# Splitting the first K products by contraction half, freeing the K/V banks later, reordering two down sets and raising a planner's latencies in a fused attention and SwiGLU kernel

## Chip, cores and metric

One core of one Trainium2 chip. The metric is the device time of one execution, in microseconds (us). Each kernel was run several times and timed beside the kernel before on the same chip. The profile is one traced execution; its span is about 1.7 us shorter than the time reported for that run.

## The reference

```python
x = A_x                                     # [1, 2048, 1024] bf16
xn = _layernorm(x)                          # no scale, no bias
s = linear_attention(xn, A_wqkv) @ A_wo     # 32 heads of 32; phi(t) = t+1 if t>0 else exp(t), + 1e-6
                                            # kv = sum phi(k) v, z = sum phi(k), o = phi(q) kv / (phi(q) z)
g = silu((silu(xn @ w_gate) * (xn @ w_up)) @ w_down)     # inner width 3584
return x + s * g
```

## The kernel before

The kernel is written as a list of operations with their reads and writes. A small planner simulates the five engines and emits each engine's instructions in the order in which they would start in that simulation. An engine then executes its list strictly in order. So a constant of the planner, such as a latency, changes no arithmetic, but it changes who stands in front of whom in each queue.

The large products are done by a seven-product scheme on half blocks (steps 1 to 7 below), with sums and differences of blocks made by VectorE (DVE); results leave the PSUM banks through DVE or ScalarE (ACT). The stages in order are: K and V products of 16 row tiles with the K/V sums accumulated in three PSUM banks; then two passes over half of the rows each, with query sets, gate/up sets and four down sets. A down set interleaves the steps D of the feed-forward product with the steps S of the attention product. S needs a 512 KB slice of the attention matrix, which is reloaded from DRAM for each down set into a single buffer.

```python
LAT = {"pe": 0.22, "act": 0.2, "dve": 0.2, "pool": 0.2}     # planner: result visible this late
...
def mm_cost(mms):
    return sum(max(r.shape[-1] / 2400.0 + 0.0012, 0.03) for (_, _, r, _, _) in mms)
...
# tile i: bn_stats x2, aggr, +eps on DVE; rstd on Pool; normalise on DVE for i < 2, on ACT after that
# t_tile(0): eight transposes on PE, first half copied out by ACT, second half by DVE:
if q == 0:
    act([bank_r[b]], [xr], dst[:, k0:k0 + n], pb, ACT.Identity)
else:
    dve([bank_r[b]], [xr], lambda h, ...: h.tensor_copy(dst[:, k0:k0 + n], pb), n * 128)
...
def p_piece(i, w, j):                       # one K or V product of row tile i: 8 matmuls of 512 columns
    b = balloc()
    mms = [(ps[b][:, :], xt_ap(i, kt), KVV[w]["R%d%d" % (kt // 4, j)][0][:, kt % 4, :], kt == 0, kt == KT - 1)
           for kt in range(KT)]
    pe_mm([xt_r(i), KVV[w]["R0%d" % j][1], KVV[w]["R1%d" % j][1]], [bank_r[b]], mms)
...
for n, (fn, args) in enumerate(((x_load, (0,)), (x_load, (1,)), (wkv_load, (0, 1)), (wkv_load, (0, 0)),
                                (x_load, (2,)), (wkv_load, (1, 1)), (x_load, (3,)), (wkv_load, (1, 0)))):
    ...                                     # wkv_load(w, j) asks for two blocks of 512 KB
...
def m_load(c):                              # slice c of the attention matrix, always into the same place
    raw = W.at(MR, 4 * KB, FP16)...
    dma([named("mscr", c // 2)], [rr], raw, m_v[:, :, c * 256:(c + 1) * 256], dsem("mld"), 512 * KB)
...
if first:                                   # down set c == 0
    seq = "D1 D5 D6 D2 D7 S1 S5 D3 S2 S6 D4 S7 S3 S4"
else:
    seq = "S1 S5 S2 S6 D1 S7 S3 D5 S4 D6 D2 D7 D3 D4"
...
# first query set of the first pass: kv_done re-arms the three K/V banks by writing to them with PE
q_pair(p, n, st, ((1, kv_done), (9, kvt)) if (p, n) == (0, 0) else ())
```

Of the kernel before, what the change touches and what calls it, by code (L numbers as in the profile page):

```python
# [14 lines left out]
KB = 1024  # L15
# [15 lines left out]
class Plan:  # L31
# [1 line left out]


    ENGS = ("pe", "act", "dve", "pool", "sp")
    LAT = {"pe": 0.22, "act": 0.2, "dve": 0.2, "pool": 0.2}

    def __init__(self, window, lead):
        self.ops = []
# [180 lines left out]
def build_kernel(nc, A_x, A_wqkv, A_wo, B_w_gate, B_w_up, B_w_down, out, WINDOW=6, NWARM=14, NPE=4, LEAD=12.0):  # L220
    S, D, FF = 2048, 1024, 3584
    NT, KT, NG, NPAIR = 16, 8, 8, 14
# [4 lines left out]
    wqkv_v = A_wqkv.rearrange("(kt p) c -> p kt c", p=128)  # L227
# [5 lines left out]
    with ExitStack() as es:  # L233
# [70 lines left out]
        MM = 0.2137  # L304

        def mm_cost(mms):
            return sum(max(r.shape[-1] / 2400.0 + 0.0012, 0.03) for (_, _, r, _, _) in mms)

        def pe_mm(reads, writes, mms):
            return PL.op("pe", reads, writes, partial(_mm_group, mms), mm_cost(mms))  # L310
# [220 lines left out]
            xslot[i] = s  # L531
            dma([], [s.r], s.ap(), xf[i * 128:(i + 1) * 128, :], dsem("x%d" % s.k), 256 * KB).urgent = 10.0

        def wkv_load(w, j):
            for k in range(2):
                ap, r = kvblock(w, KB_OF[k, j])
                c0 = 1024 * (1 + w) + j * 512
                dma([], [r], ap, wqkv_v[:, 4 * k:4 * k + 4, c0:c0 + 512], dsem("wkv%d%d%d" % (w, j, k)), 512 * KB)

        xnslot = {}  # L540

# [102 lines left out]

        def p_piece(i, w, j):
            b = balloc()
            mms = [(ps[b][:, :], xt_ap(i, kt), KVV[w]["R%d%d" % (kt // 4, j)][0][:, kt % 4, :], kt == 0, kt == KT - 1)
                   for kt in range(KT)]
            pe_mm([xt_r(i), KVV[w]["R0%d" % j][1], KVV[w]["R1%d" % j][1]], [bank_r[b]], mms)
            if w == 0:  # L650
                k_evac(i, j, ps[b][:, :], bank_r[b], "ps")
            else:
                v_evac(i, j, ps[b][:, :], bank_r[b])
            bfree(b)
# [47 lines left out]
                st.direct = direct  # L702
            return st

        for n, (fn, args) in enumerate(((x_load, (0,)), (x_load, (1,)), (wkv_load, (0, 1)), (wkv_load, (0, 0)),
                                        (x_load, (2,)), (wkv_load, (1, 1)), (x_load, (3,)), (wkv_load, (1, 0)))):
            k = len(PL.ops)
            fn(*args)
            for o in PL.ops[k:]:
                o.urgent = 60.0 - 2 * n  # L710
        ln_tile(0)
        t_tile(0)
        ln_tile(1)
        p_piece(0, 0, 1)
        t_tile(1)
        p_piece(1, 0, 1)
        x_load(4)
        x_load(5)
        p_piece(0, 0, 0)
        ln_tile(2)  # L720
        p_piece(1, 0, 0)
        t_tile(2)
        combos(KVV[0])
        p_piece(0, 1, 1)
        ln_tile(3)
        p_piece(1, 1, 1)
        t_tile(3)
        combos(KVV[1])
        p_piece(0, 1, 0)
        for b in tb:  # L730
            rearm(b)
        p_piece(1, 1, 0)
        fill = deque([partial(a_tile, 0), partial(a_tile, 1)])
        stats_of = {1: x_sums(1)}
        todo = [(u, w) for u in range(1, NT // 2) for w in range(2)]
# [310 lines left out]

        out_evs = []

        def d_set(p, c, Sx, mstat, first):
            gv, sv, xo = {}, {}, {}  # L1050

            def fin(i, j):
                if (i, j) not in gv or (i, j) not in sv:
                    return
                g, s = gv[i, j], sv[i, j]
                tt([g.r, s.r], [g.r], g.ap(FP16), g.ap(FP16), s.ap(FP16), ALU.mult, True)
                row = p * 1024 + j * 512
                if j not in xo:
                    q = xo_ring.take()
                    xo[j] = (q, [])  # L1060
                    xv = q.ap().rearrange("p (m n) -> p m n", n=256)
                    dma([], [q.r], xv, xf[row:row + 512, c * 256:(c + 1) * 256].rearrange("(m p) n -> p m n", p=128),
                        dsem("xo%d" % q.k), 256 * KB)
                q, seen = xo[j]
                xv = q.ap().rearrange("p (m n) -> p m n", n=256)

                def done():
                    seen.append(i)
                    if len(seen) == 2:
                        dma([q.r], [], of[row:row + 512, c * 256:(c + 1) * 256].rearrange(  # L1070
                            "(m p) n -> p m n", p=128), xv, dsem("oo%d" % q.k), 256 * KB)

                def turn_dma():
                    o = pt_ring.take()
                    oa = o.ap(FP16).rearrange("p (m n) -> p m n", n=128)
                    PL.op("sp", [g.r], [o.r], lambda h: h.dma_start_transpose(oa, g.ap(FP16)), 0.08,
                          sem=dsem("tp%d" % o.k), nbytes=200 * KB)
                    tt([o.r, q.r], [q.r], xv[:, :, i * 128:i * 128 + 128], oa, xv[:, :, i * 128:i * 128 + 128], ALU.add,
                       True)
                    done()  # L1080

                def turn():
                    if not tbank:
                        tbank.append(balloc())
                    b = tbank[0]
                    pb = ps[b][:, 0:256].bitcast(FP16).rearrange("p (m n) -> p m n", n=128)
                    pe_tr([g.r, ident_r], [bank_r[b]], [(pb[:, m, :], g.ap(FP16)[:, m * 128:(m + 1) * 128], ident[:, :])
                                                           for m in range(4)])
                    tt([bank_r[b], q.r], [q.r], xv[:, :, i * 128:i * 128 + 128], pb[:, :, :],
                       xv[:, :, i * 128:i * 128 + 128], ALU.add)  # L1090
                    done()
                if (p, c) == (1, 3):
                    defer(2, turn)
                else:
                    turn_dma()

            def keep(store, func):
                def f(i, j, ap, r, bank):
                    s = fin_ring.take()
                    store[i, j] = s  # L1100
                    act([r], [s.r], s.ap(FP16), ap, func, "ps" if bank is not None else "sb")
                    fin(i, j)
                return f

            def dops(m):
                wv, wr = Sx[m]
                parts = []

                def with_t4():
                    for n in range(0, NPAIR, 2):  # L1110
                        t = t4_ring.take()
                        tv = t.ap(FP16).rearrange("p (n t) -> p n t", t=512)
                        r10, t2 = hb2(n, "R10"), hb2(n, "T2")
                        tt([r10[1], t2[1]], [t.r], tv, r10[0], t2[0], ALU.subtract, True)
                        yield [(wv[:, n + q, :], tv[:, q, :]) for q in range(2)], [wr, t.r]
                if m == 4:
                    return NPAIR, with_t4()
                nm = XOF[m]
                for n in range(NPAIR):
                    ap, r = hb(n, nm)  # L1120
                    parts.append(([(wv[:, n, :], ap)], [wr, r]))
                merged = []
                for q in range(0, NPAIR, 7):
                    merged.append((sum((x[0] for x in parts[q:q + 7]), []), [r for x in parts[q:q + 7] for r in x[1]]))
                return NPAIR, merged

            dset = Set(dops, keep(gv, ACT.Silu), dd_ring)
            sset = xset(mstat, 0, QV, keep(sv, ACT.Identity), dd_ring)
            if first:
                seq = "D1 D5 D6 D2 D7 S1 S5 D3 S2 S6 D4 S7 S3 S4"  # L1130
            else:
                seq = "S1 S5 S2 S6 D1 S7 S3 D5 S4 D6 D2 D7 D3 D4"
            for w in seq.split():
                (dset if w[0] == "D" else sset).step(int(w[1]))
                tick()
# [22 lines left out]
        for p in range(2):  # L1158
            for k, n in order:
                st = got.pop((k, p, n))  # L1160
                if k == "q":
                    q_pair(p, n, st, ((1, kv_done), (9, kvt)) if (p, n) == (0, 0) else ())
                else:
                    at = ()
                    if 2 <= n <= 3:
                        at = tuple((4 + 6 * h, partial(normalise_part, p, n - 2, h)) for h in range(2))
                    gu_pair(p, n, st, at)
                pump(2)
                if p == 0 and n < 2 and k == "g":
                    for _ in range(8):  # L1170
                        if mb:
                            m_build(*mb.popleft())
                if (k, n) == ("g", 1):
                    recip(p)
            pq_load(p)
            for c in range(4):
                Sx = wd_load(c)
                ms = m_load(c)
                d_set(p, c, Sx, ms, c == 0)
            if p == 0:  # L1180
                combos(XV[1])
                gate[0] = 1
                raw_ring.k = cmb_ring.k = 0
                pump(2)
# [69 lines left out]
```

## Time and profile before

| | before |
|---|---|
| time, median of the first 3 runs | 753.27 us |
| span of the profile | 752.4 us |
| PE busy | 737.5 us |
| PE idle (span minus busy) | 14.9 us |
| DVE busy | 545.1 us |

The busy line and the chain of waits on the profile's page say that TensorE (PE) is the bound. The columns of the first line are busy us, share of the span, and instructions; PEld is PE loading weights, POOL is GpSimd, SPq and DVEq are the queues of SyncE and DVE:

```profile
PE 737.5 (98%) x3553; PEld 333.6 (44%) x3566; DVE 545.1 (72%) x1010; ACT 322.2 (43%) x532; POOL 13.4 (2%) x35
...
PE 90%; DMA 3%; DVE 3%; ACT 2%; issue 1%; SPq 0%; POOL 0%; DVEq 0%
```

No change that leaves the matmuls alone can win more than the idle time of PE. The waits of PE, by whom it waited for (total us, times, longest), show where a part of it is:

```profile
PE ps L209 <- DVE ps L329: 2.3, 3, 0.9
PE ps L209 <- DMA H<-in_A_wqkv_dram: 1.5, 1, 1.5
...
PE ps L209 <- ACT X L322: 1.2, 1, 1.2
PE ps L209 <- DVE H L791: 0.9, 1, 0.9
PE ps L209 <- DMA W<-m_scratch: 0.8, 2, 0.5
```

The timeline of PE gives the places. A row is: start, us, engine, line, operation, operands, count, and in brackets the idle time just before it with what ended it.

```profile
1.43 6.14 PE L209 MATMUL ps<-TM,ident 128*128 128x512 f16 x14 [1.43 <-POOL ident L372]
7.37 0.64 PE L216 MATMUL ps<-ident,W 128*128 128x128 f16 x8
9.51 1.89 PE L209 MATMUL ps<-H,X 128*128 128x512 bf16 x8 [1.50 <-DMA H<-in_A_wqkv_dram]
11.23 0.61 PE L216 MATMUL ps<-ident,W 128*128 128x128 f16 x8
13.00 5.35 PE L209 MATMUL ps<-H,X 128*128 128x512 bf16 x23 [1.16 <-ACT X L322]
...
126.25 0.40 PE L209 MATMUL ps<-ones,ident 128*128 128x128 f16 x4 [0.93 <-DVE H L791]
...
213.50 114.14 PE L209 MATMUL ps<-X,W 128*128 128x512 f16 x528 [0.86 <-DVE ps L329]
358.39 3.63 PE L209 MATMUL ps<-X,W 128*128 128x512 f16 x16 [0.52 <-DMA W<-m_scratch]
444.68 1.04 PE L209 MATMUL ps<-X,W 128*128 128x512 f16 x4 [0.65 <-DVE ps L329]
```

The first row is a warm-up of 14 products without use. Then come the transposes of row tile 0, and at 9.51 the first K product, which waited for its weights. Tile 1's transposes follow, and at 13.00 the next product waited for their copy. At 126.25 the re-arming of a K/V bank waited for DVE to read the sums out of it. At 358.39 the second down set waited for the slice of the attention matrix.

### The profile page before, as it was taken

How to read it: one execution, taken by the hardware profiler on the slowest of the kernel's cores; microseconds unless marked ns; L12 is line 12 of the kernel's file. 1: busy time of each engine (PE TensorE's matmuls, PEld its weight loads, DVE VectorE, ACT ScalarE, POOL GpSimd, SP SyncE). 2: the span in 40 equal slices, each digit the busy share in tenths (PEclk: the TensorE clock that was granted, in tenths of full speed). 3: DMA queues.
4: the chain of work that ended last, by engine and by line, in shares of the span. 5: the costliest groups of instructions: out<-in, count | busy, mean ns of one | idle time of the engine just before them, and what ended most of it. 6: DMA issues, size and time to landing. Idle time of an engine off the chain costs nothing.

```text
span 752.4 us, 9403 instructions
## 1 busy us (share of the span) xinstructions
PE 737.5 (98%) x3553; PEld 333.6 (44%) x3566; DVE 545.1 (72%) x1010; ACT 322.2 (43%) x532; POOL 13.4 (2%) x35
## 2 busy tenths in 40 slices
PE   7999999999999999999999999999999999999997
PEld 3444444434444444444444444344444444444443
DVE  5999857668788776876465677888867778466363
ACT  2776653575473343413232265446634333232231
POOL 2111000000000000000000000000000000000000
PEclk9999999999999999999999999999999999999999
DMA  9344223532674333344826653327642345346740
GB/s 300 91 90 93 43 56 107 174 99 85 196 217 136 83 86 106 105 140 126 202 67 173 166 121 85 107 65 201 191 112 59 109 119 177 98 112 150 195 104 29
DMA packets 166861, 93.55 MB, mean 124 GB/s; under 512 B 31392, under 2 KB 162720, under 8 KB 166816
## 3 DMA queue, kind: packets, MB, share of 16 engines
q1 hardware_dynamic: 166816, 92.95, 45.2%
q8 instruction: 28, 0.46, 0.3%
q14 instruction: 17, 0.14, 0.1%
HBM read 75.50 MB, written 10.62 MB: 114 GB/s over the span
## 4 chain that ended last, share of the span: by engine, by line
PE 90%; DMA 3%; DVE 3%; ACT 2%; issue 1%; SPq 0%; POOL 0%; DVEq 0%
PE ps L209 90%; DMA W<-in_B_w_up_dram 1%; DMA W<-m_scratch 1%; DMA H<-in_A_wqkv_dram 1%; DVE H L329 1%; ACT TM L322 1%; ACT H L322 1%; SPq L332 0%; DVE W L329 0%; DVE TM L329 0%; ACT L322 0%; PE ps L216 0%; ACT W L322 0%; DVE ps L329 0%; POOL rstd L551 0%
## 5 line engine op out<-in xcount | busy, mean ns | idle before, releaser
L209 PE MATMUL ps<-X,W 128*128 128x512 f16 x1504 | 347.0, 379 | 3.1 <-DVE ps L329 2.3
L322 ACT ACTIVATE TM<-ps 128x512 f32<-128x512 f32 (+1 forms) x275 | 161.6, 595 | 177.2 <-PE ps L209 172.8
L209 PEld LDWEIGHTS ps<-X,W 128*128 128x128 f16 (+1 forms) x1504 | 144.5, 98 | 178.3 <-DVE ps L329 4.2
L209 PE MATMUL ps<-H,W 128*128 128x512 f16 (+1 forms) x891 | 203.4, 379 | 0.3
L329 DVE TENSOR_TENSOR W<-W 128x1024 f16<-128x1024 bf16 (+3 forms) x224 | 134.1, 630 | 5.5 <-DMA W<-in_B_w_up_dram 2.9
L209 PEld LDWEIGHTS ps<-H,W 128*128 128x128 f16 (+1 forms) x896 | 87.2, 98 | 103.6 <-DVE ps L329 0.2
L209 PE MATMUL ps<-P,W 128*128 128x512 f16 x512 | 123.0, 379 | 0.0
L329 DVE TENSOR_TENSOR ps<-ps,TM 128x512 f32<-128x512 f32 x94 | 65.6, 698 | 66.6 <-PE ps L209 66.2
L329 DVE TENSOR_TENSOR TM<-ps,TM 128x512 f32<-128x512 f32 (+1 forms) x91 | 61.6, 677 | 60.8 <-PE ps L209 58.1
L322 ACT ACTIVATE ps<-ps 128x512 f32<-128x512 f32 x94 | 55.0, 585 | 95.4 <-PE ps L209 94.6
L322 ACT ACTIVATE TM<-TM 128x512 f16<-128x512 f32 (+1 forms) x61 | 37.8, 620 | 133.5 <-DVE TM L329 132.4
L209 PEld LDWEIGHTS ps<-P,W 128*128 128x128 f16 (+1 forms) x512 | 49.2, 98 | 58.9
L329 DVE TENSOR_TENSOR H<-ps,TM 128x512 f16<-128x512 f32 (+1 forms) x91 | 62.5, 690 | 14.2 <-PE ps L209 14.0
L329 DVE TENSOR_TENSOR H<-H 128x1024 f16<-128x1024 f16 (+2 forms) x82 | 50.8, 634 | 3.1 <-PE ps L209 1.9
L329 DVE TENSOR_TENSOR TM<-TM 128x512 f16<-128x512 f16 (+1 forms) x60 | 25.1, 422 | 29.8 <-DMA TM<-TM 18.5
L209 PE MATMUL ps<-H,X 128*128 128x512 bf16 (+1 forms) x133 | 32.2, 379 | 3.5 <-DMA H<-in_A_wqkv_dram 1.5
L616 DVE TENSOR_SCALAR TM<-TM 128x512 f16<-128x512 f16 x64 | 17.7, 290 | 16.4 <-ACT TM L322 16.3
L322 ACT ACTIVATE H<-ps 128x512 bf16<-128x512 f32 (+2 forms) x42 | 24.2, 615 | 10.3 <-PE ps L209 10.3
L329 DVE TENSOR_TENSOR W<-H 128x1024 f16<-128x1024 f16 x38 | 25.6, 688 | 0.8 <-PE ps L209 0.5
L209 PE MATMUL ps<-H,P 128*128 128x512 bf16 (+1 forms) x93 | 22.8, 379 | 0.2
L209 PE MATMUL ps<-W 128*128 128x512 f16 x76 | 21.8, 379 | 0.0
L322 ACT ACTIVATE H<-H,zc 128x512 bf16<-128x512 bf16 x32 | 20.9, 712 | 0.4 <-DMA H<-r_scratch 0.4
(71 smaller groups left out, 294.6 us busy)
## 6 DMA issues: line engine op xcount, KB each, us to landing
W<-in_B_w_gate_dram SPq DMA_DIRECT2D x28, 512.0 KB, 3.9
W<-in_B_w_up_dram SPq DMA_DIRECT2D x28, 512.0 KB, 5.2
W<-in_B_w_down_dram SPq DMA_DIRECT2D x16, 896.0 KB, 6.5
W<-in_A_x_dram SPq DMA_DIRECT2D x16, 256.0 KB, 2.9
H<-in_A_wqkv_dram SPq DMA_DIRECT2D x8, 512.0 KB, 8.1
W<-in_A_wqkv_dram SPq DMA_DIRECT2D x8, 512.0 KB, 4.9
H<-r_scratch SPq DMA_DIRECT2D x32, 128.0 KB, 3.7
q_scratch<-H SPq DMA_DIRECT2D x8, 512.0 KB, 3.9
```

Source lines behind the costliest of these rows:

```text
L209: last = h.matmul(o, l, r, start=st, stop=sp, skip_group_check=True)
L322: return PL.op("act", reads, writes, lambda h: h.activation(o, i, func, **kw), nel(o) / 1200.0 + (0.055 if src == "ps" else 0.095))
L329: return dve(reads, writes, lambda h: h.tensor_tensor(o, a, b, op), nel(o), 1.92 if fast else 0.96)
L616: dve([e.r], [b.r], lambda h: h.tensor_scalar(ba, ea, 1.0, EPS_PHI, ALU.min, ALU.add), 512, 2.6)
```

## The change

There are four parts. They are called head, kv, seq and lat below.

- head: each block of the first weights is asked for on its own, the first half of the first weights ahead of row tile 1; a product becomes two groups of four matmuls, each waiting only for its own half; both K products of tile 0 come before those of tile 1.
- kv: the K/V banks are re-armed after step 4 of the first query set's order instead of step 1.
- seq: the second down set starts with D1, so that the slice for S1 has time to land.
- lat: the planner's latencies and matmul cost are raised.

```diff
-    LAT = {"pe": 0.22, "act": 0.2, "dve": 0.2, "pool": 0.2}
+    LAT = {"pe": 0.25, "act": 0.3, "dve": 0.3, "pool": 0.3}
...
-            return sum(max(r.shape[-1] / 2400.0 + 0.0012, 0.03) for (_, _, r, _, _) in mms)
+            return sum(max(r.shape[-1] / 2400.0 + 0.0026, 0.03) for (_, _, r, _, _) in mms)
...
-            mms = [(ps[b][:, :], xt_ap(i, kt), KVV[w]["R%d%d" % (kt // 4, j)][0][:, kt % 4, :], kt == 0, kt == KT - 1)
-                   for kt in range(KT)]
-            pe_mm([xt_r(i), KVV[w]["R0%d" % j][1], KVV[w]["R1%d" % j][1]], [bank_r[b]], mms)
+            for k in range(2):
+                ap, r = KVV[w]["R%d%d" % (k, j)]
+                pe_mm([xt_r(i, 4 * k, 4), r], [bank_r[b]],
+                      [(ps[b][:, :], xt_ap(i, 4 * k + q), ap[:, q, :], k + q == 0, k + q == 4) for q in range(4)])
...
-        for n, (fn, args) in enumerate(((x_load, (0,)), (x_load, (1,)), (wkv_load, (0, 1)), (wkv_load, (0, 0)),
-                                        (x_load, (2,)), (wkv_load, (1, 1)), (x_load, (3,)), (wkv_load, (1, 0)))):
+        for n, (fn, args) in enumerate(((x_load, (0,)), (wkv_load, (0, 1, 0)), (x_load, (1,)), (wkv_load, (0, 1, 1)),
+                                        (wkv_load, (0, 0, 0)), (wkv_load, (0, 0, 1)), (x_load, (2,)), ...
...
         p_piece(0, 0, 1)
+        p_piece(0, 0, 0)
         t_tile(1)
         p_piece(1, 0, 1)
...
-        p_piece(0, 0, 0)
+        p_piece(1, 0, 0)          # and V likewise: (0,1,1) (1,1,1) (0,1,0) (1,1,0), each one place earlier
...
-            if first:
-                seq = "D1 D5 D6 D2 D7 S1 S5 D3 S2 S6 D4 S7 S3 S4"
-            else:
-                seq = "S1 S5 S2 S6 D1 S7 S3 D5 S4 D6 D2 D7 D3 D4"
+            seq = ("D1 D5 D6 D2 D7 S1 S5 D3 S2 S6 D4 S7 S3 S4", "D1 S1 D5 S5 S2 D6 S6 D2 S7 S3 D7 S4 D3 D4",
+                   "S1 S5 S2 S6 D1 S7 S3 D5 S4 D6 D2 D7 D3 D4")[min(c, 2)]
...
-                    q_pair(p, n, st, ((1, kv_done), (9, kvt)) if (p, n) == (0, 0) else ())
+                    q_pair(p, n, st, ((4, kv_done), (9, kvt)) if (p, n) == (0, 0) else ())
```

More of the change, by code (lines that the diff above doesn't have):

```diff
@@ L532, in x_load, with wkv_load @@
             dma([], [s.r], s.ap(), xf[i * 128:(i + 1) * 128, :], dsem("x%d" % s.k), 256 * KB).urgent = 10.0
-        def wkv_load(w, j):
-            for k in range(2):
-                ap, r = kvblock(w, KB_OF[k, j])
-                c0 = 1024 * (1 + w) + j * 512
-                dma([], [r], ap, wqkv_v[:, 4 * k:4 * k + 4, c0:c0 + 512], dsem("wkv%d%d%d" % (w, j, k)), 512 * KB)
+        def wkv_load(w, j, k):
+            ap, r = kvblock(w, KB_OF[k, j])
+            c0 = 1024 * (1 + w) + j * 512
+            dma([], [r], ap, wqkv_v[:, 4 * k:4 * k + 4, c0:c0 + 512], dsem("wkv%d%d%d" % (w, j, k)), 512 * KB)
         xnslot = {}
@@ L703, in kv_set @@
             return st
-        for n, (fn, args) in enumerate(((x_load, (0,)), (x_load, (1,)), (wkv_load, (0, 1)), (wkv_load, (0, 0)),
-                                        (x_load, (2,)), (wkv_load, (1, 1)), (x_load, (3,)), (wkv_load, (1, 0)))):
+        for n, (fn, args) in enumerate(((x_load, (0,)), (wkv_load, (0, 1, 0)), (x_load, (1,)), (wkv_load, (0, 1, 1)),
+                                        (wkv_load, (0, 0, 0)), (wkv_load, (0, 0, 1)), (x_load, (2,)),
+                                        (wkv_load, (1, 1, 0)), (wkv_load, (1, 1, 1)), (x_load, (3,)),
+                                        (wkv_load, (1, 0, 0)), (wkv_load, (1, 0, 1)))):
             k = len(PL.ops)
@@ L718, in build_kernel @@
         x_load(5)
-        p_piece(0, 0, 0)
+        p_piece(1, 0, 0)
         ln_tile(2)
-        p_piece(1, 0, 0)
+        p_piece(0, 1, 1)
         t_tile(2)
         combos(KVV[0])
-        p_piece(0, 1, 1)
+        p_piece(1, 1, 1)
         ln_tile(3)
-        p_piece(1, 1, 1)
+        p_piece(0, 1, 0)
         t_tile(3)
         combos(KVV[1])
-        p_piece(0, 1, 0)
+        p_piece(1, 1, 0)
         for b in tb:
             rearm(b)
-        p_piece(1, 1, 0)
         fill = deque([partial(a_tile, 0), partial(a_tile, 1)])
@@ L1047, in build_kernel, with d_set @@
         out_evs = []
-        def d_set(p, c, Sx, mstat, first):
+        def d_set(p, c, Sx, mstat):
             gv, sv, xo = {}, {}, {}
@@ L1178, in build_kernel @@
                 ms = m_load(c)
-                d_set(p, c, Sx, ms, c == 0)
+                d_set(p, c, Sx, ms)
             if p == 0:
```

## The prediction

> **What bounds the kernel.** TensorE. The busy table gives PE 737.5 of 752.4 us (98%) at granted clock 0.999; the chain of waits is 90% matmul. DVE is busy 72%, ACT 43%. No matmul is removed, so only the 14.9 us in which PE is idle (2%) can be won. A 512-column matmul takes 0.216 us in the chain of waits (650 in 140.49); the Trainium skill, "TensorE: Matmul & The Clock Gate", section "Back-to-back issue gap", gives 512/2.4 + 2.5 ns = 215.8 ns: the trace agrees, PE runs at its rate, and the planner's new matmul cost is the truer one.
>
> **Where PE idles** (PE timeline and waits): 1.43 at launch; 1.50 before the first K product at 9.51 (waits for the second half of its weights, landing 9.26; the activations were there at 8.47); 1.16 at 13.00 (copy of tile 1's transposes); 0.19, 0.47, 0.33 up to 27; 0.22 at 122; 0.93 at 126.25 (re-arming a K/V bank, behind DVE reads of the sums, eight of 0.27); 0.76, 0.86, 0.65 at 159.6, 213.5, 444.7 (a DVE sum, twice behind ACT table loads of 1.28); 0.52 at 358.4 and 0.32 at 667.35 (reload of the attention matrix for the second down set, 4.3 us from issue); the rest mostly in the tail after 744.
>
> **What the change does.**
> 1. Head: the weights' first half is asked for second instead of third, and a product's first four matmuls need only that half. I expect the first K product at about 8.5, and product (0,0,0) to fill the 1.16 hole while tile 1 is normalised later. DMA moves about 360 GB/s from 6 to 18 us already, so not everything comes earlier. DVE is 97% busy from 15 to 30 and 96% from 30 to 60, but idle over 4 us between 8 and 15, and the combinations can start earlier as their readers end earlier. Worth 1.0 to 2.5, say 1.7 us, all on the critical path.
> 2. K/V banks re-armed after step 4 of the first query set instead of step 1: the DVE reads are over by then. Saves 0.9; five banks stay free, enough for two interleaved sets.
> 3. The second down set begins with D1 (14 matmuls, 3.0 us), so the reload lands before S1: 0.9 over both passes, with the restart of the weight loads.
> 4. The planner's latencies (0.2 to 0.3) and matmul cost change the order on every engine. It may hide some of the 2.3 us of DVE waits, or open small ones: 0.5 saved, plus or minus 1.2.
>
> Sum: 1.7 + 0.9 + 0.9 + 0.5 = 4.0 us, so 753.3 - 4.0 = **749.3 us**, range 746.8 to 751.8. Chances: faster by over 2% 0.01 (it would need all of PE's idle time), within 2% 0.98, slower by over 2% 0.01.
>
> **What would show it right.** PE busy stays within 0.5 us of 737.5, PE idle falls to about 11; first K product before 9.0; no 0.9 wait at the re-arming near 125; no wait of PE for the attention matrix; the stages from 213 on start about 2.5 us earlier, those after the second down set about 3.
>
> **What would make it wrong.** DVE, nearly full from 15 to 60, becomes the limit, so PE starts early and waits later; tile 1 or 2 lands too late behind the weights; fewer free banks in the first query set make PE wait; D and S alternating in the second down set make PE wait for ACT copies or DVE sums; reordering opens new waits in the steady stages.

## More of the kernel before

One more view matters later: what DVE did before tile 0 could be normalised. L547 and L548 are statistics, L549 and L550 their end, L556 the normalisation.

```profile
4.51 0.68 DVE L547 BATCH_NORM_STATS2 stats<-W 128x6 f32<-128x512 bf16 x1
5.10 0.19 DVE L549 BATCH_NORM_AGGREGATE mv<-stats 128x2 f32<-128x12 f32 x1
5.21 0.64 DVE L548 BATCH_NORM_STATS2 stats<-W 128x6 f32<-128x512 bf16 x1
5.76 0.14 DVE L550 TENSOR_SCALAR veps<-mv 128x1 f32<-128x1 f32 x1
...
6.58 1.17 DVE L556 TENSOR_SCALAR W<-W,mv,rstd 128x1024 f16<-128x1024 bf16 x2 [0.30 <-POOL rstd L551]
```

The statistics at 4.51 and 5.21 belong to tile 1. They stand between those of tile 0 (3.31 and 3.92) and the end of tile 0's, at 5.76.

## The result and the profile after

| | before | after |
|---|---|---|
| time, median of 6 runs each | 753.49 us (752.38 to 754.82) | 748.13 us (747.71 to 748.32) |
| span of the profile | 752.4 us | 746.2 us |
| PE busy | 737.5 us | 736.1 us |
| PE idle | 14.9 us | 10.1 us |

The ratio of after to before is 0.9926, 95% interval 0.9913 to 0.9939. Ratios here are the mean time of one kernel's runs over that of the other's of the same rounds, so not quite the ratio of the medians quoted. A later set of runs, on chip 8, gave 0.9942 (0.9928 to 0.9957). The gain is real and 3.7 to 5.4 us in the medians.

The page after, the same two lines:

```profile
PE 736.1 (99%) x3553; PEld 333.2 (45%) x3566; DVE 545.3 (73%) x1010; ACT 321.7 (43%) x532; POOL 17.0 (2%) x35
...
PE 94%; DVE 2%; ACT 2%; DMA 1%; issue 0%; SPq 0%
```

The waits of PE after. The wait for the attention matrix (m_scratch) is gone, the one for the K/V sums (now L793, the same code) is 0.2:

```profile
PE ps L209 <- DVE ps L329: 1.2, 2, 0.8
...
PE ps L209 <- ACT X L322: 0.7, 2, 0.5
...
PE ps L209 <- DMA H<-in_A_wqkv_dram: 0.3, 1, 0.3
...
PE ps L209 <- DVE H L793: 0.2, 1, 0.2
```

The timeline of PE after:

```profile
1.43 4.70 PE L209 MATMUL ps<-TM,ident 128*128 128x512 f16 x14 [1.43 <-POOL ident L372]
6.39 0.62 PE L216 MATMUL ps<-ident,W 128*128 128x128 f16 x8 [0.26 <-DVE W L555]
7.48 1.91 PE L209 MATMUL ps<-H,X 128*128 128x512 bf16 x8 [0.47 <-ACT X L322]
9.72 1.04 PE L209 MATMUL ps<-H,X 128*128 128x512 bf16 x4 [0.34 <-DMA H<-in_A_wqkv_dram]
10.82 0.62 PE L216 MATMUL ps<-ident,W 128*128 128x128 f16 x8
11.28 1.03 PE L209 MATMUL ps<-H,X 128*128 128x512 bf16 x4
12.55 5.35 PE L209 MATMUL ps<-H,X 128*128 128x512 bf16 x23 [0.25 <-ACT X L322]
...
125.43 0.91 PE L209 MATMUL ps<-ones,ident 128*128 128x128 f16 x8 [0.16 <-DVE H L793]
...
439.71 1.04 PE L209 MATMUL ps<-X,W 128*128 128x512 f16 x4 [0.43 <-DVE ps L329]
```

And DVE in front of tile 0's normalisation (L546 to L549 are the statistics, L555 the normalisation):

```profile
4.71 0.21 DVE L548 BATCH_NORM_AGGREGATE mv<-stats 128x2 f32<-128x12 f32 x1
4.96 0.15 DVE L549 TENSOR_SCALAR veps<-mv 128x1 f32<-128x1 f32 x1
5.79 0.55 DVE L555 TENSOR_SCALAR W<-W,mv,rstd 128x1024 f16<-128x1024 bf16 x1 [0.68 <-POOL rstd L550]
6.25 0.68 DVE L546 BATCH_NORM_STATS2 stats<-W 128x6 f32<-128x512 bf16 x1
```

Tile 1's statistics now start at 6.25, behind tile 0's normalisation, which starts at 5.79 instead of 6.58.

Adding up the idle gaps of PE over 0.08 us by place, from the two timelines, gives this table.

| place | before | after |
|---|---|---|
| launch | 1.43 | 1.43 |
| from the transposes of tile 0 to 45 us | 3.65 (1.50, 1.16, 0.19, 0.47, 0.33) | 1.99 (0.26, 0.47, 0.34, 0.25, 0.23, 0.09, 0.35) |
| end of the K/V sums and re-arming | 1.15 (0.22, 0.93) | 0.16 |
| DVE sum behind ACT's table load, near 157 to 160 | 0.76 | 0.77 |
| DVE sum at 213.5 | 0.86 | 0 |
| attention matrix, both passes | 0.84 (0.52, 0.32) | 0 |
| DVE sum at the start of the second pass | 0.65 | 0.43 |
| tail | 1.48 (0.33, 1.15) | 1.14 (0.21, 0.93) |

The gaps fall from 10.8 to 5.9 us; the idle time that is left over in both (4.1 and 4.2 us) is mostly the end after the last matmul. The rest of the 6.2 us of span is busy time, 1.4 us, and all of that is the warm-up: 14 products in 6.14 us before, in 4.70 after. Without it PE is busy for 731.4 us in both. Three things in this comparison are chance of the one profile of before. The gap at 213.5 is absent from all 13 other traces, also from those of kernels with only the head, only kv or only seq changed. The chain of waits of before follows it back to a load of `w_up` that took 8.83 us to land (the median of such loads in this trace is 5.2):

```profile
200.28 8.83 DMA W<-in_B_w_up_dram
```

The warm-up took between 4.53 and 6.14 us over the 14 traces, with the same 14 products. And the wait of 1.50 for the first weights is in part chance: of the five traces with the old head, only before and only_lat (1.33) have it. In only_kv, only_seq and without_head the weights had landed; the first K product waited 0.54 to 0.64 for the DVE copy of tile 0 and started at 8.30 to 8.76 instead of 9.51. The line of without_head:

```profile
8.30 1.89 PE L209 MATMUL ps<-H,X 128*128 128x512 bf16 x8 [0.54 <-DVE X L589]
```

The profiled run of before itself took 754.16 us, more than the 753.27 of the runs beside it. So the profile's 6.2 us overstates what the change gave, and only runs can say what each part is worth.

### The profile page after: what moved, and what is told of

It reads as the page before. It is cut to its first block, busy times and chain, and to the rows that moved or that the text cites. A ratio compares the mean times of both kernels' runs of the same rounds, so it can differ in the third digit from the quotient of the medians.

```text
span 746.2 us, 9376 instructions
## 1 busy us (share of the span) xinstructions
PE 736.1 (99%) x3553; PEld 333.2 (45%) x3566; DVE 545.3 (73%) x1010; ACT 321.7 (43%) x532; POOL 17.0 (2%) x35
## 4 chain that ended last, share of the span: by engine, by line
PE 94%; DVE 2%; ACT 2%; DMA 1%; issue 0%; SPq 0%
PE ps L209 94%; DMA W<-in_A_x_dram 1%; ACT H L322 1%; ACT TM L322 0%; SPq L332 0%; DVE TM L329 0%; ACT L322 0%; DVE W L329 0%; DVE H L793 0%; PE ps L216 0%; ACT ps L322 0%; DVE ps L329 0%; DVE H L329 0%; DVE TM L615 0%; DVE H L616 0%
## 5 line engine op out<-in xcount | busy, mean ns | idle before, releaser
L209 PE MATMUL ps<-H,X 128*128 128x512 bf16 (+1 forms) x133 | 32.5, 379 | 1.8 <-ACT X L322 0.7
```

The lines of the kernel that those rows point to most:

```text
L209: last = h.matmul(o, l, r, start=st, stop=sp, skip_group_check=True)
```

## The experiments

Each part was first applied alone to the kernel before, then taken away alone from the kernel after. The sets ran on chips 0 (the four only_ runs), 8 (after_again and the next three) and 10 (the last four); each is compared with the kernel before in the same set. The kernel after was not run on chip 10, so the distance of the last four runs from it is worked out from ratios.

| run | median | before beside it | ratio (95% interval) |
|---|---|---|---|
| only_head | 751.26 | 752.65 | 0.9981 (0.9968 to 0.9993) |
| only_kv | 751.40 | 752.65 | 0.9982 (0.9970 to 0.9994) |
| only_seq | 752.23 | 752.65 | 1.0010 (0.9989 to 1.0031) |
| only_lat | 753.09 | 752.65 | 1.0006 (0.9994 to 1.0018) |
| after_again | 748.24 | 751.89 | 0.9942 (0.9928 to 0.9957) |
| without_head | 750.64 | 751.89 | 0.9979 (0.9966 to 0.9992) |
| without_lat | 750.03 | 751.89 | 0.9967 (0.9955 to 0.9980) |
| without_kv | 749.20 | 751.89 | 0.9960 (0.9946 to 0.9974) |
| without_seq | 749.41 | 752.29 | 0.9955 (0.9942 to 0.9969) |
| x1_first | 749.19 | 752.29 | 0.9956 (0.9943 to 0.9968) |
| unsplit | 749.13 | 752.29 | 0.9957 (0.9944 to 0.9969) |
| act_copy | 750.28 | 752.29 | 0.9969 (0.9957 to 0.9982) |

All outputs are right.

### only_head

Edit: the head hunks of the diff above (loads, split products, order of products), applied to the kernel before.

```diff
+            for k in range(2):
+                ap, r = KVV[w]["R%d%d" % (k, j)]
+                pe_mm([xt_r(i, 4 * k, 4), r], ...)      # and the load order and product order of the change
```

> The kernel before with only the head changed (order of the first loads, first products split by contraction half, their new order). Theory: the head alone is worth 2.0 us of waits (first K product at 7.5 instead of 9.5, later holes smaller), and another 0 to 1.4 of it depends on when the warm-up products end. Time 2.0 to 3.5 us below the kernel before; the last K/V sums end about 2 us earlier (before: 122.7), while the 0.9 wait at the re-arming near 124 and the waits for the attention matrix (0.5 and 0.3) are still there. Rival (DVE-bound from 15 to 60): first product early, but the K/V stage ends less than 0.7 us earlier and the time falls by less than 0.7.

Measured: 1.4 us under before in the medians, less than the 2.0 to 3.5 expected, more than the rival's 0.7. The first K product starts at 7.83 and the 0.93 wait at the re-arming is still there, as are those for the attention matrix (0.41 and 0.27). But the waits that follow between 11 and 32 us are not smaller, as had been expected: 2.2 us (0.61, 0.25, 0.24, 0.24, 0.40, 0.45) where before has 2.15 (1.16, 0.19, 0.47, 0.33). Under the old latencies, the new head runs into new waits on DVE and ACT. It is worth less alone than its start suggests.

### only_kv

```diff
-                    q_pair(p, n, st, ((1, kv_done), (9, kvt)) if (p, n) == (0, 0) else ())
+                    q_pair(p, n, st, ((4, kv_done), (9, kvt)) if (p, n) == (0, 0) else ())
```

> The kernel before with only the re-arming of the K/V banks moved from step 1 to step 4. Theory: the 0.93 us wait of PE before the re-arming goes, nothing replaces it: time 0.7 to 1.1 us below the kernel before. Rival: with five banks for longer, PE waits for a bank in the steps between: gain under 0.4.

Measured: 1.25 us under before. In its trace both gaps near 122 and 126 (0.22 and 0.93, 1.15 together) are gone and none stands in their place. The rival, too few free banks, falls.

### only_seq

Edit: the seq hunk of the diff above, applied to the kernel before.

```diff
+            seq = (..., "D1 S1 D5 S5 S2 D6 S6 D2 S7 S3 D7 S4 D3 D4", ...)[min(c, 2)]
```

> The kernel before with only the order of products in the second down set changed. Theory: the waits of PE for the attention matrix (0.52 at 358 and 0.32 at 667) go: time 0.7 to 1.1 us below the kernel before, PE idle elsewhere unchanged. Rival: the alternation of D and S opens waits of PE for ACT or DVE inside the set, gain under 0.4.

Measured: the trace shows no wait for the attention matrix in either pass, and no new one in the down sets, as expected. The time does not show it. Two of the six runs took 756.17 and 755.89 us at a mean granted clock of 0.994; the other four are 751.34 to 752.65. With all six the result is unclear; the time of this part is better read from without_seq.

### only_lat

```diff
-    LAT = {"pe": 0.22, "act": 0.2, "dve": 0.2, "pool": 0.2}
+    LAT = {"pe": 0.25, "act": 0.3, "dve": 0.3, "pool": 0.3}
-            return sum(max(r.shape[-1] / 2400.0 + 0.0012, 0.03) ...
+            return sum(max(r.shape[-1] / 2400.0 + 0.0026, 0.03) ...
```

> The kernel before with only the planner's latencies and matmul cost changed. Theory: this alone removes the 0.86 wait near 213.5 (PE for a DVE sum, because DVE does a multiplication of the normalising part first), and leaves the waits of the head, the re-arming and the attention matrix: time 0.5 to 1.3 us below the kernel before. Rival: the removal of that wait came with the changed position of the banks, and this alone gives nothing (within 0.4).

Measured: 0.4 us above before, with an interval that holds 1. So the expectation was wrong and the 0.86 at 213.5 proves nothing, since it is missing from every other trace. The second pass and the tail do gain (0.43 instead of 0.65 at 444.56, 0.20 and 0.93 instead of 0.33 and 1.15), but the head loses. The PE timeline of this run:

```profile
20.84 0.62 PE L216 MATMUL ps<-ident,W 128*128 128x128 f16 x8 [0.77 <-ACT W L322]
...
28.54 0.40 PE L209 MATMUL ps<-ones,ident 128*128 128x128 f16 x4 [0.29 <-ACT X L322]
...
33.58 0.82 PE L209 MATMUL ps<-H,X 128*128 128x512 bf16 x3 [0.72 <-ACT ps L322]
...
40.50 1.68 PE L209 MATMUL ps<-H,W 128*128 128x512 f16 x7 [0.17 <-DVE ps L329]
```

These are 1.95 us of waits where before has 0.99 (0.19, 0.47, 0.33): the order that the new constants make does not suit the old head.

### after_again

The kernel after, unchanged.

> The kernel after, unchanged, as the yardstick for the runs beside it. Expected 748.1 (747.7 to 748.4) where the kernel before has 752.5 to 753.5; PE idle about 10 us. If the long warm-up of the first profile of before (14 products in 6.14 us against 4.70) is chance, the warm-up here may end anywhere between 6.0 and 7.6.

Measured: 748.24 us, as expected. Its gaps are those of the first profile of after, place by place, within 0.08 us, but for the 0.26 before the transposes, which is missing. The warm-up took 5.56 us here and the first K product began at 7.89.

### without_head

Edit: the head hunks of the diff reversed on the kernel after.

```diff
-            for k in range(2):
-                ap, r = KVV[w]["R%d%d" % (k, j)]
-                pe_mm([xt_r(i, 4 * k, 4), r], ...)      # and loads and order of products as before
```

> The kernel after with the head of before put back. If the parts only add up: slower than the kernel after by what the head gave alone, 1.4 us. Theory: the new latencies fit only the new head (with the old head they gave new waits of 0.77, 0.29, 0.73 and 0.16 between 20 and 41 us), so head and latencies gain together: 2.5 to 4 us slower than the kernel after, that is 750.6 to 752.1, with waits of over 1.5 us in all between 18 and 41.

Measured: 2.4 us slower than the kernel after of the same set. The waits of only_lat are back at 19.8, 27.5, 32.5 and 39.4 (0.78, 0.29, 0.72, 0.17 in the brackets of its timeline, over 1.5 in all as expected). The 2.4 is just under the 2.5 to 4 of the theory and clearly above the 1.4 of the sum rule.

### without_lat

Edit: the lat hunks reversed on the kernel after (the diff of only_lat, from plus to minus).

> The kernel after with the old latencies and matmul cost. If the parts only add up: 0.4 us faster than the kernel after, as the new latencies alone cost 0.4. Theory: with the new head they pay: 1.0 to 2.0 us slower than the kernel after, of which about 0.9 in waits between 10 and 32 us, 0.2 near 440 and 0.35 in the tail.

Measured: 1.8 us slower than the kernel after, although the same constants alone had cost 0.4. The gaps agree: 7.4 us in all against 5.7 in after_again. By place the extra is 0.65 between 18 and 32 us (0.24, 0.23, 0.40, 0.45 against 0.23, 0.09, 0.35), 0.45 between 9 and 12 (perhaps chance, see without_seq), 0.2 at 440 and 0.35 in the tail. The waits between 18 and 32 stand in only_head too (0.24, 0.24, 0.40, 0.45), so they belong to the new head with the old constants, and not to kv or seq. There head and lat gain together. The last two differences are the same in all nine traces with the new constants against all five with the old, whatever the head.

### without_kv

```diff
-                    q_pair(p, n, st, ((4, kv_done), (9, kvt)) if (p, n) == (0, 0) else ())
+                    q_pair(p, n, st, ((1, kv_done), (9, kvt)) if (p, n) == (0, 0) else ())
```

> The kernel after with the K/V banks re-armed after step 1 again. Theory: a wait of 0.9 before the re-arming comes back and the rest stays: 0.8 to 1.3 us slower than the kernel after. Rival: with the new latencies the order has changed enough that the position hardly matters: within 0.4.

Measured: 0.96 us slower than the kernel after. The waits of PE show the re-arming again:

```profile
PE ps L209 <- DVE H L793: 0.9, 1, 0.9
```

Its trace also has a wait of 0.84 at 9.52 for the DVE copy of tile 0's second half; see without_seq.

### without_seq

Edit: the seq hunk reversed on the kernel after.

```diff
-            seq = (..., "D1 S1 D5 S5 S2 D6 S6 D2 S7 S3 D7 S4 D3 D4", ...)[min(c, 2)]
+            if first: ...        # second down set as before: "S1 S5 S2 S6 D1 S7 S3 D5 S4 D6 D2 D7 D3 D4"
```

> The kernel after with the old order of products in the second down set. Theory: the waits of PE for the attention matrix come back in both passes (0.4 to 0.6 and 0.3): 0.6 to 1.0 us slower than the kernel after (0.9926 and 0.9942 of before in two sets of runs). Rival: with the new latencies only the first of them comes back, as in the run with the latencies alone (0.59 at 358, none at 667): 0.3 to 0.6 slower.

Measured: ratio 0.9955 where after_again has 0.9942, worked out on 752 us about 1.0 us slower; the intervals overlap, so this is a best estimate. In the trace the wait for the attention matrix is back with 0.55 at 355.6 and 0.13 at 663.8. The first agrees with both expectations; the second has nearly gone, as the rival said.

```profile
355.56 2.76 PE L209 MATMUL ps<-X,W 128*128 128x512 f16 x12 [0.55 <-DMA W<-m_scratch]
```

This trace also caught something that the single profile of after does not show. DVE and PE near the start:

```profile
8.14 0.69 DVE L546 BATCH_NORM_STATS2 stats<-W 128x6 f32<-128x512 bf16 x1 [1.59 <-DMA W<-in_A_x_dram]
8.75 0.68 DVE L547 BATCH_NORM_STATS2 stats<-W 128x6 f32<-128x512 bf16 x1
9.34 0.41 DVE L588 COPY X<-ps 128x512 f16<-128x512 f16 x1
...
9.89 1.02 PE L209 MATMUL ps<-H,X 128*128 128x512 bf16 x4 [1.17 <-DVE mv L548]
```

Tile 1 landed late (6.4 us after its issue; 4.0 in the first profile of after). DVE stood idle for 1.59 us in front of tile 1's statistics, and the copy of tile 0's second half (L588), whose input had been there since about 7.2, stood behind them in the queue. The second half of the first K product needs that copy and started at 9.89; the trace puts the end of its wait down to the DVE instruction after the copy (L548). This did not come from seq: without_kv and without_lat show it too, with 0.84 and 0.44, and there the copy itself (L588) is named.

### x1_first

```diff
-        for n, (fn, args) in enumerate(((x_load, (0,)), (wkv_load, (0, 1, 0)), (x_load, (1,)), (wkv_load, (0, 1, 1)),
+        for n, (fn, args) in enumerate(((x_load, (0,)), (x_load, (1,)), (wkv_load, (0, 1, 0)), (wkv_load, (0, 1, 1)),
```

> The kernel after with tile 1 asked for before the first half of the weights, as in the kernel before; split and order of products stay. Theory: half of the earlier start of the first K product comes from DVE: with tile 1 landing later, its statistics no longer stand in front of tile 0's normalisation. With tile 1 first again, the planner puts them there again: tile 0's transposes start about 0.8 later (7.1 to 7.3 instead of 6.4 to 6.6), the first K product at 8.3 to 8.6 instead of 7.5 to 7.9, time 0.3 to 1.0 us above the kernel after. Rival: only the landing of weights counts, and the start moves by less than 0.3.

Measured: the theory holds. Tile 1's statistics are again in front of tile 0's normalisation, and the first K product starts 0.6 to 1.0 us later than in the two traces of the kernel after:

```profile
5.40 0.64 DVE L547 BATCH_NORM_STATS2 stats<-W 128x6 f32<-128x512 bf16 x1
5.96 0.14 DVE L549 TENSOR_SCALAR veps<-mv 128x1 f32<-128x1 f32 x1
...
6.77 1.17 DVE L555 TENSOR_SCALAR W<-W,mv,rstd 128x1024 f16<-128x1024 bf16 x2 [0.30 <-POOL rstd L550]
...
8.46 1.04 PE L209 MATMUL ps<-H,X 128*128 128x512 bf16 x4 [0.47 <-ACT X L322]
```

The ratio, 0.9956 against 0.9942 of after_again, is about 1 us on 752; the intervals overlap. In return the holes at 9 to 13 us are gone, as tile 1 is ready in time, but a wait of 1.09 for tile 3's normalisation appears at 25.4, so the time does not measure the earlier start alone. The start does: 8.46 is where the old head starts too when its weights are in time (8.30 to 8.76), so against those traces, as far as they show, the gain in the start comes from the order on DVE alone.

### unsplit

```diff
-            for k in range(2):
-                ap, r = KVV[w]["R%d%d" % (k, j)]
-                pe_mm([xt_r(i, 4 * k, 4), r], [bank_r[b]], ...)
+            mms = [...]                          # all eight matmuls
+            pe_mm([xt_r(i), KVV[w]["R0%d" % j][1], KVV[w]["R1%d" % j][1]], [bank_r[b]], mms)
```

> The kernel after with every first product again one group of eight matmuls that waits for both halves of its weights; loads and order of products stay. Theory: the split lets the first product start 0.7 us before the second half lands, and the second product do half of its work before its second half lands: 0.5 to 1.2 us slower than the kernel after, first K product at 8.2 to 9.3. Rival: PE waits for the following landing anyway, so the split is worth under 0.3.

Measured: ratio 0.9957, so about 1.1 us slower than after_again by the same working, within the range of the theory. The first product now waits for the second half of its weights:

```profile
8.36 1.89 PE L209 MATMUL ps<-H,X 128*128 128x512 bf16 x8 [1.17 <-DMA H<-in_A_wqkv_dram]
```

Its gaps add up to 6.4 us against 5.7, which is 0.7 of the difference. The intervals overlap here too.

### act_copy

An attempt at a version that beats both: the copy that could be held behind tile 1's statistics goes to ACT.

```diff
-                if q == 0:
+                if True:                         # both halves of tile 0's transposes copied by ACT
                     act([bank_r[b]], [xr], dst[:, k0:k0 + n], pb, ACT.Identity)
```

> An attempt to beat both: the kernel after with the second half of tile 0's transposes copied by ACT too, not by DVE. In two profiles with the new head PE waited 0.43 and 0.83 us for this DVE copy, because DVE's queue has tile 1's statistics in front of it and those wait for tile 1's landing. Theory: no such wait any more, first product of eight matmuls without a hole; 0 to 0.5 us faster than the kernel after, on average 0.2, and no slow start in any profile. Rival: the planner's new order costs as much as this gains: same within 0.3 or slower.

Measured: 750.28 us, ratio 0.9969. That is slower than the kernel after, by about 2 us on after_again's ratio. The first product does run without a hole from 7.59, so the aimed-at wait is gone. But the planner made another order, in which tile 3 is normalised later:

```profile
26.38 0.62 PE L216 MATMUL ps<-ident,W 128*128 128x128 f16 x8 [1.03 <-ACT W L322]
```

Together with 0.60 at 10.17 and 0.44 at 32.01, the gaps sum to 7.0 us, in the fastest of its six runs (749.32). No version tried beats the kernel after.

## Why the prediction was right

The time was 748.13 us where 749.3 was predicted, with a range of 746.8 to 751.8; the repeat was 748.24. The bound, the size of the gain and "within 2%" hold. Point by point:

- What bounds the kernel: right. All idle time of PE was 14.9 us, and the change took about a third of it.
- Step 1, the head: 1.7 us predicted. Alone it gave 1.4, taken away it cost 2.4. The hole of 1.16 was filled as predicted; 0.25 is left of it. The first K product came 0.6 to 1.0 us earlier than predicted: at 7.48, and 7.89 in the repeat, instead of "about 8.5". The prediction took the 8.47 at which tile 0's activations had been ready as given. It did not see that this moment was itself late because tile 1's statistics stood in front of tile 0's normalisation, and that asking for tile 1 later moves them behind it; x1_first shows this. That 1.7 still fits is partly luck: its largest term, the wait of 1.50 for weights, is missing from three of the five traces with the old head, and a gain that was not foreseen took its place. The fear that DVE would swallow the gain shows only in part: between 18 and 32 us PE waits for DVE and ACT 1.3 us with the new head alone (0.24, 0.24, 0.40, 0.45), 1.0 in before and 0.7 with the change complete.
- Step 2, the K/V banks: 0.9 predicted, 1.25 measured alone and 0.96 when taken away; right. The wait of 0.22 for the last V copy went with it, which was not foreseen.
- Step 3, the second down set: 0.9 predicted. The waits of 0.52 and 0.32 are gone in every trace that has the new order. They came to 0.84 in before only; in the four other traces with the old order (only_head, only_kv, only_lat, without_seq) they are 0.6 to 0.7. The time, about 1.0 us from without_seq, agrees but is not resolved from noise.
- Step 4, the planner's constants: "0.5 saved, plus or minus 1.2" was mis-sized as one number. Alone the constants cost 0.4 us (not clear of noise), in the whole they save 1.8. The gaps say why: 0.57 us, in the second pass and the tail, goes with the constants in every trace; between 18 and 42 us they add 0.96 with the old head (1.95 against 0.99) and take away 0.65 with the new one (0.67 against 1.32).
- The sum: 4.0 predicted. The parts alone add up to 2.6 us (1.4 + 1.25 + 0.4 - 0.4, medians); the whole gave 3.7 beside after_again and 5.4 in the first set. Most of the difference lies in head and lat, which fit each other. So the sum came out near although two of its four terms were made of other things than predicted; that part is luck.
- The check on later stages ("the stages from 213 on start about 2.5 us earlier, those after the second down set about 3"): the first H,W products after the gate and up stage start at 323.11 instead of 327.48, the one at the start of the second pass that waits for DVE at 439.71 instead of 444.68. That is 4.4 and 5.0 us. Without the two chances of before (1.44 of warm-up, 0.86 at 213.5) it is 2.1 and 2.7, near the forecast.
- The check "PE busy within 0.5 us of 737.5" failed: 736.1. The 1.44 us are the warm-up products, which count as busy whether they run slowly or fast: in the trace of before their weight loads are 0.43 us apart to the end, in that of after about 0.22 from 4.39 us on. The page "Trainium Kernel Development and Optimization" of the Trainium skill, section "Performance Expectations", calls matmul busy time a bad metric for how close a kernel is to its roofline, because matmuls are pipelined. PE busy moved by 1.4 us with no work changed.

What stays open: which of the two constants of lat matters; what the new order of the first products is worth, which was never taken away alone as the load order and the split were; and how much of the 5.4 us in the first set, against 3.7 in the second, is the chip and how much the scatter of the kernel before (751.44 to 754.82 over all sets; the kernel after stays within 747.71 to 748.68).

## What to carry to other kernels

When an engine executes its queue in order, ask of each load not only who waits for its data but what stands behind the instruction that will wait for it; moving one load can free, or hold, work that never touches it. Where a planner or a compiler orders the queues, the worth of a cost constant depends on the rest of the program: measure parts alone and taken away from the whole, because here the same constants added about 1.0 us of waits near the start with one head and removed about 0.65 with another. When only a per cent of idle time is left, one profile of each kernel is not enough: a gap of 0.86 us, 1.4 us of warm-up and part of a 1.50 us wait for weights differed here by chance.

## What the Trainium skill lacked or had wrong

- "TensorE: Matmul & The Clock Gate", section "What's actually happening": it says that the array runs at half clock for about 3.4 us of sustained work and that this varies from run to run. The same 14 warm-up products took 4.53 to 6.14 us over 14 traces. In the trace of before, weight loads are still 0.43 us apart at 6.52, 5.1 us after the first product. That is longer than the 3.4 us, but not outside what the section says of the spread: it counts 6, 11 or 14 slow matmuls for one kernel. Not said there: the profile's granted clock reads 1.00 in each microsecond from 2 to 7, in before as in after, so this column does not show the slow products.
- "TensorE: Matmul & The Clock Gate", section "Back-to-back issue gap", from which the prediction took its 215.8 ns: the section calls that formula the gap of an isolated matmul, and gives about 131 ns for N=512 in a sustained stream with a weight load for each matmul. Here 650 such products in a row took 140.49 us, 0.216 each: the formula holds for the stream, and the 131 does not.
- "DMA: Bandwidth & Descriptors", section "Latency and other measured facts", gives no spread for a load behind others. The load of row tile 1, third to be issued in each run with the new load order, landed 4.0 to 6.4 us after its issue in eight traces. With the DVE queue of this kernel that was worth up to 1.17 us of PE.
- No page covers slow single runs of one core: four runs lay 2.5 to 4 us above the median of their kernel in the same set (only_seq 756.17 and 755.89 at a mean granted clock of 0.994; before 754.38 and 754.77 at 0.996). As an estimate from these numbers, 0.005 and 0.003 of 752 us below the usual 0.999 are 3.8 and 2.3 us, which is about the whole of it. No run here shows what lowered the clock.
